# Attention with a maxout layer behind it on one core: q and k transposed by DMA from group 6 on, and the value product moved beside a score visit

## The chip, the core and the metric

The kernel runs on one of the eight cores of a Trainium2 chip. The time is the device time of one execution in microseconds (us), and lower is better. A core has five engines that run their own instruction streams and wait for one another through semaphores: TensorE (PE in the profile, its weight loads PEld), VectorE (DVE), ScalarE (ACT), GpSimd (POOL) and SyncE (SP). [...]

## The reference

Eight batches, twelve heads, 448 positions, head size 64. Softmax has one extra term in its denominator. What comes out is put side by side over the heads and goes through a layer that takes the largest of three products, and through an output product:

```
scores = (1/8) * q @ k.T            # (8, 12, 448, 448)
m      = max(scores)                # per row
e      = exp(scores - m)
attn   = e / (sum(e) + exp(-m) + 1e-9)
x      = attn @ v                   # put together as (3584, 768)
h      = max(x @ w1, x @ w2, x @ w3)
out    = h @ w_out                  # (3584, 768), float32
```

Times m, numerator and denominator become exp(scores) and sum(exp(scores)) + 1; the kernel computes those, without the maximum.

## The kernel before

**Groups.** The work is cut into 24 groups of four heads, three groups to a batch. The order of all instructions is the order in which the code calls them; nothing reorders it. One turn of the main loop (`for i in range(NI)`) does, on TensorE, the four score visits of group i, the value product of group i-1, the transposes of group i+1, and in between as many pieces of the maxout layer as a budget in columns allows (`moe`, line 281).

**One group.** `load_group` (line 76) has POOL load q, k and v as fp16, 112 positions to a chunk, into a pool of five buffers each. `pair_qk` (line 123) copies k and q of two heads side by side on VectorE, four copies to a group. `transpose_pair` (line 138) turns such a pair on TensorE: eight transposes of 112 by 128 into one PSUM bank, `trT`, and one VectorE copy to `qkT` in SBUF. `scores_visit` (line 152) does four products of 64 by 128 by 448 into `stp`, and ScalarE takes two exponentials of them into `eT`. `av_group` (line 179) does 48 products with 32 columns each: 16 with a matrix of ones for the denominator and 32 with v; ScalarE takes the logarithm and the exponential that make the reciprocal `rb`, and VectorE multiplies into `xT` (line 206, two per group).

**The maxout layer.** As soon as a batch's third group has its `xT`, `add_pieces` puts 18 pieces `up_piece` (six products of 128 by 128 by 448, then one VectorE copy or maximum into `hT`) and six or eight pieces `out_piece` (six products with 384 columns, one VectorE scaling into `o_sb`, and stores from SP) on a list. They fill the gaps of the next three groups.

**What is shared.** TensorE works in three arrangements of its array: whole (layer, transposes), two row halves (scores), four column strips (value product). PSUM has four single banks (`bank1`) for `trT`, `av`, `p_i` and `op_ps`, and two double ones for the scores. In the first turns POOL also loads the four weight matrices, between the groups.

Of the kernel before, what the change touches and what calls it, by code (L numbers as in the profile page):

```python
# [14 lines left out]
ts = bass.ts  # L15

MMDT = FP16
# [4 lines left out]
def kernel(  # L22
# [11 lines left out]
    nc = tc.nc  # L34

    B, H, S, D = q.shape
    NTOK, DM = out.shape
    DFF = moe_w1.shape[1]
    SC = 112
    NCH = S // SC  # L40
# [10 lines left out]
            name=nc.get_next_instruction_name(),  # L51
# [5 lines left out]

    cpool = ctx.enter_context(tc.tile_pool(name="const", bufs=1))
    ld_pool = ctx.enter_context(tc.tile_pool(name="ld", bufs=5))
    p16_pool = ctx.enter_context(tc.tile_pool(name="p16", bufs=2))  # L60
    att_pool = ctx.enter_context(tc.tile_pool(name="att", bufs=4))
    e_pool = ctx.enter_context(tc.tile_pool(name="e", bufs=2))
    small = ctx.enter_context(tc.tile_pool(name="small", bufs=2))
    xt_pool = ctx.enter_context(tc.tile_pool(name="xt", bufs=2))
# [11 lines left out]
    def load_group(i, which="qkv", step=GH):  # L76
        b, g = groups[i]
        tiles = raw.setdefault(i, {})
        for name in which:
            tiles[name] = ld_pool.tile(  # L80
                [SC, GH, NCH, D], MMDT, tag="ld_" + name, name="ld_" + name
            )
        for h0 in range(0, GH, step):
            for name in which:
                src = {"q": q, "k": k, "v": v}[name][b].rearrange(
                    "(g h) (p c) d -> g p h (c d)", g=NG, c=NCH
                )[g]
                nc.gpsimd.dma_start(  # L88
                    out=tiles[name][:, h0 : h0 + step].rearrange("p h c d -> p h (c d)"),
                    in_=src[:, h0 : h0 + step],  # L90
                )
# [19 lines left out]
    def load_weight(i):  # L111
        w = (moe_w1, moe_w2, moe_w3, moe_w_out)[i]
        for g in range(NG):
            if i < 3:
                src = w.rearrange("(g p hf) f -> g p hf f", g=NG, hf=2)[g]
            else:
                src = w.rearrange("(g hf p) f -> g p hf f", g=NG, hf=2)[g]
            nc.gpsimd.dma_start(out=w_sb[i][:, 2 * g : 2 * g + 2, :], in_=src)


    state = {}

    def pair_qk(i):
        qf, kf = raw[i].pop("q"), raw[i].pop("k")
        qk16 = []
        for pr in range(GH // 2):
            q16 = p16_pool.tile([SC, NCH, 2, D], MMDT, tag=f"q16_{pr}", name=f"q16_{pr}")
            k16 = p16_pool.tile([SC, NCH, 2, D], MMDT, tag=f"k16_{pr}", name=f"k16_{pr}")
            nc.vector.tensor_copy(
                out=k16, in_=kf[:, 2 * pr : 2 * pr + 2].rearrange("p h c d -> p c h d")  # L130
            )
            nc.vector.tensor_copy(
                out=q16, in_=qf[:, 2 * pr : 2 * pr + 2].rearrange("p h c d -> p c h d")
            )
            qk16.append((q16, k16))
        state[i] = {"qk16": qk16, "qkT": []}

    def transpose_pair(i, pr):
        st = state[i]
        q16, k16 = st["qk16"][pr]  # L140
        trT = ps1.tile([128, 2, S], MMDT, tag="bank1", name="trT")
        for n, t16 in enumerate((k16, q16)):
            for c in range(NCH):
                nc.tensor.transpose(  # L144
                    out=trT[:, n, ts(c, SC)], in_=t16[:, c, :, :],
                    identity=ident16[0:SC, 0:SC],
                )
        qkT = att_pool.tile([2 * D, 2 * S], MMDT, tag="qkT", name="qkT")
        nc.vector.tensor_copy(out=qkT, in_=trT.rearrange("p n s -> p (n s)"))  # L149
        st["qkT"].append(qkT)  # L150

    def scores_visit(i, pr, cs):
        st = state[i]
        if "eT" not in st:
            st["eT"] = e_pool.tile([SC, GH, NCH, S], MMDT, tag="eT", name="eT")
        qkT = st["qkT"][pr]
        stps = []
        for c in cs:
            stp = ps2.tile([128, 2, 512], FP32, tag="bank2", name="stp")
            for hh in range(2):  # L160
                nc.tensor.matmul(  # L161
                    out=stp[:, hh, 0:S],
                    lhsT=qkT[hh * D : hh * D + D, c * SC : c * SC + 128],
                    rhs=qkT[hh * D : hh * D + D, S : 2 * S],
                    start=True,
                    stop=True,
                )
            stps.append(stp)
        for c, stp in zip(cs, stps):
            nc.scalar.activation(  # L170
                out=st["eT"][:, 2 * pr : 2 * pr + 2, c, :],
                in_=stp[0:SC, :, 0:S],
                func=AF.Exp,
                scale=scale,
            )
# [3 lines left out]
    def av_group(i):  # L179
        b, g = groups[i]  # L180
        st = state.pop(i)
        eT, v16 = st["eT"], raw[i].pop("v")
        if g == 0:
            xT[b] = xt_pool.tile([128, NDC, S], MMDT, tag="xT", name="xT")

        def col_tiled(weights):
            bank = ps1.tile([128, 512], FP32, tag="bank1", name="av")
            for c in range(NCH):
                for hh in range(GH):
                    nc.tensor.matmul(  # L190
                        out=bank[32 * hh : 32 * hh + 32, 0:S],
                        lhsT=weights(hh, c),
                        rhs=eT[:, hh, c, :],
                        start=(c == 0),
                        stop=(c == NCH - 1),
                    )
            return bank

        den = col_tiled(lambda hh, c: ones16[:, :])
        lnd = small.tile([128, S], FP32, tag="lnd", name="lnd")  # L200
        nc.scalar.activation(out=lnd, in_=den[:, 0:S], func=AF.Ln, bias=one_b)  # L201
        rb = small.tile([128, S], FP32, tag="rb", name="rb")
        nc.scalar.activation(out=rb, in_=lnd, func=AF.Exp, bias=ln_lam, scale=-1.0)  # L203
        for hf in range(2):
            num = col_tiled(lambda hh, c: v16[:, hh, c, hf::2])
            nc.vector.tensor_tensor(  # L206
                out=xT[b][:, 2 * g + hf, :], in0=num[:, 0:S], in1=rb, op=ALU.mult
            )
# [60 lines left out]
    def add_pieces(b):  # L269
        order = [(fc, i) for fc in range(NFC) for i in range(3)]  # L270
        if b == 0:
            order = [(fc, i) for i in range(3) for fc in range(NFC)]
        for fc, i in order:
            pieces.append((up_piece, (b, fc, i), NDC * (S + 6)))
        for t in range(0, 3) if b % 2 == 0 else range(3, 7):
            for nh in range(NH):
                pieces.append((out_piece, (b // 2, t, nh), NFC * (NW + 6)))
# [3 lines left out]
    def moe(cols):  # L281
        credit[0] += cols
        while pieces and credit[0] > 0:
            f, a, w = pieces.pop(0)
            f(*a)
            credit[0] -= w
        if not pieces:
            credit[0] = min(credit[0], 0.0)
# [4 lines left out]
    per_group = (3 * NFC * UP + 3.5 * NH * OUT) / NG  # L293
    av_cols = 3 * NCH * (S + 6) + 480
    tr_cols = 2 * NCH * SC
    gap = (per_group + av_cols + 2 * tr_cols) / 4
    visits = [(pr, cs) for pr in range(2) for cs in ((0, 1), (2, 3))]
    NI = len(groups)

    pair_qk(0)  # L300
    transpose_pair(0, 0)
    transpose_pair(0, 1)

    for i in range(NI):
        b, g = groups[i]
        if i == 0:
            load_weight(0)
            load_group(3, "qk")
        elif i == 1:
            load_weight(1)  # L310
            load_group(3, "v")
        elif i == 2:
            load_weight(2)
            load_group(4)
            load_weight(3)
            load_group(5)
        elif i + 3 < NI:
            load_group(i + 3)
        for vi, (pr, cs) in enumerate(visits):
            scores_visit(i, pr, cs)  # L320
            if vi == 0:
                spare = gap - av_cols
                moe(spare / 2)
                if i > 0:
                    av_group(i - 1)
                moe(spare / 2)
                if i > 0 and g == 0:
                    add_pieces(b - 1)
                if i + 1 < NI:
                    pair_qk(i + 1)  # L330
            elif vi < 3:
                moe((gap - tr_cols) / 2)
                if i + 1 < NI:
                    transpose_pair(i + 1, vi - 1)
                moe((gap - tr_cols) / 2)
            else:
                moe(gap)
    av_group(NI - 1)
    add_pieces(B - 1)
# [31 lines left out]
```

## Time and profile before

| | |
|---|---|
| three runs | 378.81, 380.77 and 381.11 us, median 380.77 |
| profiled execution | 379.41 us, its span 377.6 us |
| TensorE busy | 358.3 us, 95% of the span |
| VectorE, ScalarE busy | 194.7 and 194.5 us, 52% each |
| GpSimd busy | 59.4 us, 16% |
| loads on POOL's queue | 21.24 MB, 40.8% of the sixteen DMA engines' span |
| stores on SP's queue | 11.01 MB, 9.8% |

Busy times overlap between engines. A matmul's span in the profile is longer than the step from one matmul to the next, since they are pipelined; the chain of waits, which follows the work that ended last back to the start, gives each piece of work by what it adds to the end.

### The profile page before, as it was taken

How to read it: one execution, taken by the hardware profiler on the slowest of the kernel's cores; microseconds unless marked ns; L12 is line 12 of the kernel's file. 1: busy time of each engine (PE TensorE's matmuls, PEld its weight loads, DVE VectorE, ACT ScalarE, POOL GpSimd, SP SyncE). 2: the span in 40 equal slices, each digit the busy share in tenths (PEclk: the TensorE clock that was granted, in tenths of full speed). 3: DMA queues.
4: the chain of work that ended last, by engine and by line, in shares of the span. 5: the costliest groups of instructions: out<-in, count | busy, mean ns of one | idle time of the engine just before them, and what ended most of it. 6: DMA issues, size and time to landing. Idle time of an engine off the chain costs nothing.

```text
span 377.6 us, 7320 instructions
## 1 busy us (share of the span) xinstructions
PE 358.3 (95%) x3120; PEld 172.0 (46%) x3120; DVE 194.7 (52%) x395; ACT 194.5 (52%) x241; POOL 59.4 (16%) x92
## 2 busy tenths in 40 slices
PE   2777999999999999999999999999999999999995
PEld 1233444544445444454445544454444554445552
DVE  2233545545546546546546555455465465445553
ACT  1879464663655655555555645546555554552000
POOL 8533450220210201202202202202000000000000
PEclk9999999999999999999999999999999999999999
DMA  7999998555508625455236555077010410013005
GB/s 92 185 208 206 204 196 121 73 136 68 73 2 151 111 54 75 60 139 75 32 43 89 126 101 73 6 128 141 2 26 0 128 43 0 2 32 95 2 0 168
DMA packets 40064, 32.71 MB, mean 87 GB/s; under 512 B 2272, under 2 KB 35296, under 8 KB 40032
## 3 DMA queue, kind: packets, MB, share of 16 engines
q0 software_dynamic: 35552, 21.24, 40.8%
q1 hardware_dynamic: 4480, 11.01, 9.8%
q8 instruction: 24, 0.39, 0.5%
q14 instruction: 8, 0.07, 0.0%
HBM read 42.47 MB, written 11.01 MB: 142 GB/s over the span
## 4 chain that ended last, share of the span: by engine, by line
PE 84%; DMA 9%; ACT 2%; POOL 2%; DVE 1%; issue 1%; DVEq 0%; POOLq 0%
PE p_i L220 43%; PE op_ps L241 15%; PE av L190 11%; PE stp L161 10%; PE trT L144 4%; DMA w_123<-in_moe_w_dram 3%; DMA ld_k<-in_k_dram 3%; DMA ld_q<-in_q_dram 2%; DVE xT L206 1%; ACT eT L170 1%; ACT rb L203 1%; ACT lnd L201 1%; POOL ld_q L88 1%; POOL ld_k L88 1%; POOL ld_v L88 0%
## 5 line engine op out<-in xcount | busy, mean ns | idle before, releaser
L170 ACT ACTIVATE eT<-stp 112x896 f16<-112x896 f32 x192 | 164.9, 916 | 145.1 <-PE stp L161 145.1
L230 DVE TENSOR_TENSOR hT<-hT,p_i 128x448 f16<-128x448 f16 x96 | 59.4, 619 | 45.5 <-PE p_i L220 45.1
L206 DVE TENSOR_TENSOR xT<-av,rb 128x448 f16<-128x448 f32 x48 | 27.8, 619 | 70.8 <-ACT rb L203 64.7
L220 PE MATMUL p_i<-xT,w_122 128*128 128x448 f16 x288 | 63.0, 353 | 0.4
L220 PE MATMUL p_i<-xT,w_123 128*128 128x448 f16 x288 | 62.4, 353 | 0.0
L220 PE MATMUL p_i<-xT,w_124 128*128 128x448 f16 x288 | 62.2, 353 | 0.0
L161 PE MATMUL stp<-qkT 64*128 64x448 f16 x384 | 56.3, 364 | 4.9 <-ACT eT L170 4.8
L241 PE MATMUL op_ps<-w_125,hT 128*128 128x384 f16 x336 | 59.5, 326 | 0.0
L88 POOL DMA_DIRECT2D ld_v<-in_v_dram x24 | 16.8, 702 | 192.3 <-PE av L190 126.3
L248 DVE TENSOR_SCALAR o_sb<-op_ps 128x384 f32<-128x384 f32 x56 | 31.2, 557 | 28.5 <-PE op_ps L241 28.4
L241 PEld LDWEIGHTS <-hT 128*128 128x128 f16 x336 | 30.9, 98 | 24.8 <-issue 6.3
L190 PE MATMUL av<-eT,ld_v 112*32 112x448 f16 x768 | 41.8, 361 | 0.0
L228 DVE CAST hT<-p_i 128x448 f16<-128x448 f32 x48 | 29.7, 620 | 19.9 <-PE p_i L220 19.9
L220 PEld LDWEIGHTS <-w_123 128*128 128x128 f16 x288 | 25.9, 98 | 29.6 <-issue 9.2
L220 PEld LDWEIGHTS <-w_124 128*128 128x128 f16 x288 | 26.0, 98 | 28.7 <-issue 7.8
L220 PEld LDWEIGHTS <-w_122 128*128 128x128 f16 x288 | 26.1, 98 | 27.8 <-issue 7.0
L149 DVE COPY qkT<-trT 128x896 f16<-128x896 f16 x48 | 29.5, 615 | 3.1 <-PE trT L144 3.0
L161 PEld LDWEIGHTS <-qkT 64*128 64x128 f16 x384 | 12.0, 94 | 40.9 <-issue 40.3
L190 PEld LDWEIGHTS <-ld_v 112*32 112x32 f16 x768 | 21.0, 99 | 16.8 <-issue 1.7
L190 PE MATMUL av<-eT,ones_116 112*32 112x448 f16 x384 | 23.3, 364 | 0.0
L88 POOL DMA_DIRECT2D ld_q<-in_q_dram x25 | 17.7, 709 | 6.9 <-DMA w_124<-in_moe_w_dram 1.5
L88 POOL DMA_DIRECT2D ld_k<-in_k_dram x25 | 17.6, 703 | 4.4 <-DMA w_123<-in_moe_w_dram 1.1
(305 smaller groups left out, 142.1 us busy)
## 6 DMA issues: line engine op xcount, KB each, us to landing
ld_v<-in_v_dram POOLq DMA_DIRECT2D x24, 224.0 KB, 4.0
ld_q<-in_q_dram POOLq DMA_DIRECT2D x23, 224.0 KB, 4.9
ld_k<-in_k_dram POOLq DMA_DIRECT2D x23, 224.0 KB, 5.9
out_dram<-o_sb SPq DMA_DIRECT2D x8, 336.0 KB, 2.8
out_dram<-o_sb SPq DMA_DIRECT2D x8, 288.0 KB, 2.7
out_dram<-o_sb SPq DMA_DIRECT2D x8, 240.0 KB, 2.8
out_dram<-o_sb SPq DMA_DIRECT2D x8, 192.0 KB, 2.7
w_122<-in_moe_w_dram POOLq DMA_DIRECT2D x3, 384.0 KB, 10.7
```

What stands on the lines that cost most here:

```text
L88: nc.gpsimd.dma_start(out=tiles[name][:, h0 : h0 + step].rearrange("p h c d -> p h (c d)"), in_=src[:, h0 : h0 + step],)
L144: nc.tensor.transpose(out=trT[:, n, ts(c, SC)], in_=t16[:, c, :, :], identity=ident16[0:SC, 0:SC],)
L149: nc.vector.tensor_copy(out=qkT, in_=trT.rearrange("p n s -> p (n s)"))
L161: nc.tensor.matmul(out=stp[:, hh, 0:S], lhsT=qkT[hh * D : hh * D + D, c * SC : c * SC + 128], rhs=qkT[hh * D : hh * D + D, S : 2 * S], sta ...
L170: nc.scalar.activation(out=st["eT"][:, 2 * pr : 2 * pr + 2, c, :], in_=stp[0:SC, :, 0:S], func=AF.Exp, scale=scale,)
L190: nc.tensor.matmul(out=bank[32 * hh : 32 * hh + 32, 0:S], lhsT=weights(hh, c), rhs=eT[:, hh, c, :], start=(c == 0), stop=(c == NCH - 1),)
L206: nc.vector.tensor_tensor(out=xT[b][:, 2 * g + hf, :], in0=num[:, 0:S], in1=rb, op=ALU.mult)
L220: nc.tensor.matmul(out=p_i[:, 0:S], lhsT=w_sb[i][:, dc, ts(fc, 128)], rhs=xT[b][:, dc, :], start=(dc == 0), stop=(dc == NDC - 1),)
L228: nc.vector.tensor_copy(out=dst, in_=p_i[:, 0:S])
L230: nc.vector.tensor_tensor(out=dst, in0=dst, in1=p_i[:, 0:S], op=ALU.max)
L241: nc.tensor.matmul(out=op_ps[:, 0:NW], lhsT=hT[bp][:, fc, ts(t, 128)], rhs=wout_sb[:, fc, ts(nh, NW)], start=(fc == 0), stop=(fc == NFC - 1),)
L248: nc.vector.tensor_scalar(out=o_sb[:, ts(nh, NW)], in0=op_ps[:, 0:NW], scalar1=1.0 / LAMBDA, scalar2=None, op0=ALU.mult,)
```

## The change

For groups 6 to 23 the eight TensorE transposes per pair, the PSUM bank and the VectorE copy out of it are gone. In their place SP issues one transposing DMA per pair, from the paired copy `qk16` in SBUF straight to `qkT`, 112 by 1024 elements; it is issued two groups ahead of the score visits that read it. k and q of a pair now lie in one tile. The pools are deepened: four pairs of `qk16` instead of two, six `qkT` instead of four. Groups 0 to 5 are transposed on TensorE as before. Inside a turn two things move: `pair_qk` now stands right behind the first score visit, ahead of the value product, and in turn 4 both group 5 and group 6 are paired there; and the value product stands right ahead of the second score visit, with the first gap's layer pieces before it. The budget `gap` is smaller by the transposes that are gone.

```
-    p16_pool = ctx.enter_context(tc.tile_pool(name="p16", bufs=2))
-    att_pool = ctx.enter_context(tc.tile_pool(name="att", bufs=4))
+    p16_pool = ctx.enter_context(tc.tile_pool(name="p16", bufs=4))
+    att_pool = ctx.enter_context(tc.tile_pool(name="att", bufs=6))
...
+            qk16 = p16_pool.tile([SC, 2, NCH, 2, D], MMDT, tag="qk16", name="qk16")
+            for n, t in enumerate((kf, qf)):
+                nc.vector.tensor_copy(
+                    out=qk16[:, n],
+                    in_=t[:, 2 * pr : 2 * pr + 2].rearrange("p h c d -> p c h d"),
+                )
...
+    def dma_transpose_pair(i, pr):
+        st = state[i]
+        qkT = att_pool.tile([2 * D, 2 * S], MMDT, tag="qkT", name="qkT")
+        nc.sync.dma_start_transpose(
+            out=qkT.rearrange("p (n s) -> p n s", s=SC),
+            in_=st["qk16"][pr].rearrange("p n c h d -> p (n c h d)"),
+        )
+        st["qkT"].append(qkT)
...
+        on_pe = i + 1 < PE_TR
+        tr = tr_cols if on_pe else 0
+        gap = (per_group + av_cols + 2 * tr) / 4
         for vi, (pr, cs) in enumerate(visits):
+            if vi == 1 and i > 0:
+                av_group(i - 1)
             scores_visit(i, pr, cs)
             if vi == 0:
-                spare = gap - av_cols
-                moe(spare / 2)
-                if i > 0:
-                    av_group(i - 1)
-                moe(spare / 2)
-                if i > 0 and g == 0:
+                if on_pe:
+                    pair_qk(i + 1)
+                if i + 2 >= PE_TR and i + 2 < NI:
+                    pair_qk(i + 2)
+                    for p2 in range(2):
+                        dma_transpose_pair(i + 2, p2)
+                moe(gap - av_cols)
+            elif vi < 3:
+                if vi == 1 and i > 0 and g == 0:
                     add_pieces(b - 1)
-                if i + 1 < NI:
-                    pair_qk(i + 1)
-            elif vi < 3:
-                moe((gap - tr_cols) / 2)
-                if i + 1 < NI:
-                    transpose_pair(i + 1, vi - 1)
-                moe((gap - tr_cols) / 2)
+                moe((gap - tr) / 2)
+                if on_pe:
+                    pe_transpose_pair(i + 1, vi - 1)
+                moe((gap - tr) / 2)
```

VectorE in turn 3, where the value product of group 2 completes the first batch and group 4 is paired. Before, the two multiplications into `xT`, then the four copies of group 4, then the first layer pieces:

```order
L206 TENSOR_TENSOR xT<-av,rb 128x448 x2
L129 COPY k_0_563<-ld_k 112x512
L132 COPY q_0_562<-ld_q 112x512
L129 COPY k_1_567<-ld_k 112x512
L132 COPY q_1_566<-ld_q 112x512
L228 CAST hT<-p_i 128x448 x2
```

The same place in the changed kernel (lines are those of its own file):

```order
L129 COPY qk_497<-ld_k 112x512
L129 COPY qk_497<-ld_q 112x512
L129 COPY qk_500<-ld_k 112x512
L129 COPY qk_500<-ld_q 112x512
L212 TENSOR_TENSOR xT<-av,rb 128x448 x2
L234 CAST hT<-p_i 128x448 x2
```

The four copies, which wait for the loads of group 4, now stand ahead of the two multiplications.

SP's queue of the changed kernel from its start (before, it held the stores alone): the transposes of groups 6 and 7, the first six stores, then the transposes of group 8.

```order
L152 DMA_TRANSPOSE qkT<-qk_692 128x8x112
L152 DMA_TRANSPOSE qkT<-qk_695 128x8x112
L152 DMA_TRANSPOSE qkT<-qk_885 128x8x112
L152 DMA_TRANSPOSE qkT<-qk_888 128x8x112
L270 DMA out_dram<-o_sb 112x768
L270 DMA out_dram<-o_sb 16x768
L270 DMA out_dram<-o_sb 96x768
L270 DMA out_dram<-o_sb 32x768
L270 DMA out_dram<-o_sb 80x768
L270 DMA out_dram<-o_sb 48x768
L152 DMA_TRANSPOSE qkT<-qk_1064 128x8x112
L152 DMA_TRANSPOSE qkT<-qk_1067 128x8x112
```

A transpose that waits now holds the stores behind it, and a store that waits holds the transposes.

More of the change, by code (lines that the diff above doesn't have):

```diff
@@ L124, in pair_qk, with pe_transpose_pair @@
         qf, kf = raw[i].pop("q"), raw[i].pop("k")
-        qk16 = []
+        state[i] = {"qk16": [], "qkT": []}
         for pr in range(GH // 2):
[L127 to L138, printed above, removed]
+            qk16 = p16_pool.tile([SC, 2, NCH, 2, D], MMDT, tag="qk16", name="qk16")
[4 more added lines that the diff above has]
+                )
+            state[i]["qk16"].append(qk16)
+    def pe_transpose_pair(i, pr):
         st = state[i]
-        q16, k16 = st["qk16"][pr]
+        qk16 = st["qk16"][pr]
         trT = ps1.tile([128, 2, S], MMDT, tag="bank1", name="trT")
-        for n, t16 in enumerate((k16, q16)):
+        for n in range(2):
             for c in range(NCH):
                 nc.tensor.transpose(
-                    out=trT[:, n, ts(c, SC)], in_=t16[:, c, :, :],
+                    out=trT[:, n, ts(c, SC)], in_=qk16[:, n, c, :, :],
                     identity=ident16[0:SC, 0:SC],
@@ L295 @@
     tr_cols = 2 * NCH * SC
-    gap = (per_group + av_cols + 2 * tr_cols) / 4
     visits = [(pr, cs) for pr in range(2) for cs in ((0, 1), (2, 3))]
     NI = len(groups)
+    PE_TR = 6
     pair_qk(0)
-    transpose_pair(0, 0)
-    transpose_pair(0, 1)
+    pe_transpose_pair(0, 0)
+    pe_transpose_pair(0, 1)
     for i in range(NI):
```

## The prediction

> **What bounds the kernel now.** I read the page first: busy time, the slices, the chain of waits.
>
> ```profile
> span 377.6 us, 7320 instructions
> PE   2777999999999999999999999999999999999995
> PE 84%; DMA 9%; ACT 2%; POOL 2%; DVE 1%; issue 1%; DVEq 0%; POOLq 0%
> PE p_i L220 43%; PE op_ps L241 15%; PE av L190 11%; PE stp L161 10%; PE trT L144 4%; DMA w_123<-in_moe_w_dram 3%; DMA ld_k<-in_k_dram 3%; DMA ld_q<-in_q_dram 2%; DVE xT L206 1%; ACT eT L170 1%; ACT rb L203 1%; ACT lnd L201 1%; POOL ld_q L88 1%; POOL ld_k L88 1%; POOL ld_v L88 0%
> ```
>
> TensorE is the bound from the fifth slice on, and the transposes stand on its chain with 4%. The DMA share is at the start. I then asked for the chain in order of time, once for the start (columns: start, length, what) and once for a turn in the middle.
>
> ```profile
> 29.02 12.52 DMA ld_k<-in_k_dram
> 41.63 0.30 DVE k_0_563 L129
> 41.98 0.57 PE trT L144 x8
> 42.55 1.14 PE p_i L220 x6
> 50.95 0.48 PE stp L161 x4
> ```
>
> ```profile
> 173.06 0.40 PE trT L144 x8
> 173.46 1.14 PE p_i L220 x6
> 174.59 0.48 PE stp L161 x4
> 175.08 1.24 PE p_i L220 x6
> 176.32 0.40 PE trT L144 x8
> 176.71 1.14 PE p_i L220 x6
> ```
>
> So there are two stages. Until 41.5 us the end is set by loads: the last to matter is k of group 4, issued at 29.02 and there at 41.54. Whatever TensorE gains before that is absorbed. From 42 us on TensorE goes from piece to piece without a hole, and what is taken out of its stream comes out of the time.
>
> **The change part by part.**
>
> *TensorE without transposes.* Groups 6 to 23 are 18, with two pairs each: 36 pairs. Their transposes and copies are all that lies between 68 and 350 us (columns: stretch, its length, busy time and count for line 144; then the same for the copy of line 149):
>
> ```profile
> 68.00:350.00 282.00, 20.11 (x288) 17.72 (x288) 1.00 0.40 70
> 68.00:350.00 282.00, 22.09 (x36) 1.00 0.40 70
> ```
>
> 288 is 36 x 8. Their 20.11 us of busy time overlaps itself, so the price is the chain's: 0.40 us per pair, and a layer piece costs the same 1.14 with a transpose behind it (173.46) as behind its own kind, since both use the whole array. Pieces alternate between 0.39 and 0.40; 36 x 0.395 = 14.2 us go. The 22.1 us of VectorE copies go too, but that engine was half idle and they are worth nothing by themselves.
>
> *The value product moved.* A change of arrangement costs about 0.10: a layer piece of 1.14 is 1.24 where a score visit follows. What counts is how many there are. By the order of the two programs there are 200 changes between whole array, row halves and column strips before, and 199 after: where the product stood behind the first visit it now stands ahead of the second. That the neighbour doesn't matter the end of the loop shows:
>
> ```profile
> 335.35 3.03 PE op_ps L241 x18
> 338.38 0.48 PE stp L161 x4
> 338.87 3.03 PE op_ps L241 x18
> 341.90 0.90 PE av L190 x16
> ```
>
> 18 output products take 3.03 ahead of scores and ahead of a value product. I take zero.
>
> *VectorE's copies ahead of the multiplications.* This is a new wait. In turn 3 the trace has:
>
> ```profile
> 38.88 1.16 DVE L206 TENSOR_TENSOR xT<-av,rb 128x448 f16<-128x448 f32 x2 [4.90 <-ACT rb L203]
> 39.22 2.44 PE L220 MATMUL p_i<-xT,w_122 128*128 128x448 f16 x12
> 41.63 0.29 DVE L129 COPY k_0_563<-ld_k 112x512 f16<-112x512 f16 x1 [1.60 <-DMA ld_k<-in_k_dram]
> 41.98 0.37 PE L144 MATMUL trT<-ident_97,k_0_563 112*128 112x112 f16 x4 [0.32 <-DVE k_0_563 L129]
> 42.45 1.14 DVE L228 CAST hT<-p_i 128x448 f16<-128x448 f32 x2
> ```
>
> The multiplications finish xT of the first batch at 40.04, and TensorE does two layer pieces while VectorE waits for k of group 4. In the changed kernel the four copies stand first and VectorE takes its queue in order, so the multiplications wait for the same load. The copies take until 42.45 (where the next operation started), the two multiplications 1.16, so xT is complete at 43.61, about 43.65 for TensorE. The first piece can do its first four products before that, its sixth at 43.65; that product takes 0.19 (a sixth of 1.14), the second piece 1.14, the transposes behind it 0.39: 45.37. Before, the same point is 42.55. So +2.8 us, and nothing later gives it back, since TensorE has no holes from there on. The load itself I take as unmoved, because POOL's order of loads is the same.
>
> In turn 4, from 50.95 (then 53.8), VectorE copies groups 5 and 6. Group 6's k is there at 54.3, by the time from its issue at 43.0 to landing:
>
> ```profile
> L88 POOL DMA_DIRECT2D ld_k<-in_k_dram x1: 701/701/701, 43.0 to 43.0; - x1
> DMA to landing us min/median/max: 11.3/11.3/11.3
> ```
>
> Group 5's copies cover those 0.5 us: zero. Without the delay in turn 3 it would have been a stall of its own. Later loads are there a turn or more ahead. In turns that begin a batch the copies also pass ahead of the multiplications, but these start 3.4 us after the first visit (166.98, then 170.37, below) and the copies are done by then.
>
> ```profile
> 166.98 0.55 PE L161 MATMUL stp<-qkT 64*128 64x448 f16 x4
> 170.37 1.15 DVE L206 TENSOR_TENSOR xT<-av,rb 128x448 f16<-128x448 f32 x2 [2.72 <-ACT rb L203]
> ```
>
> In that wait TensorE stands still for about 3 us (39.98 to 43.0). At the start of the trace its products ran at half pace:
>
> ```profile
> 17.67 1.69 PE L190 MATMUL av<-eT,ones_116 112*32 112x448 f16 x16
> 27.82 0.94 PE L190 MATMUL av<-eT,ones_116 112*32 112x448 f16 x16
> ```
>
> Sixteen of the 48 products took 0.75 longer there. If the pause brings that back for the length of one value product, it costs 3 x 0.75 = 2.2 us once; below, nothing. No row has a pause of this length after full pace. I take zero, because most of the trace's holes leave the pace alone (the product at 27.82 follows a stretch in which TensorE waited for ScalarE again and again), and keep 2.2 for the range. The Trainium skill (TensorE: Matmul & The Clock Gate, Part 1) has the clock fall to half after about 3.4 us without work; by that rule this pause is just too short.
>
> *The transposing DMAs.* No row shows one. Each moves 112 x 1024 fp16, the 224 KB of one load. A turn is 14.58 us long before: turn 4 begins at 50.95 and turn 23 at 327.90 (row further down), 276.95 / 19. Two pairs fewer make it 13.79. Group 6's transposes are issued at about 55.9 (53.8, the visit, eight copies) and read about 82, two turns after turn 4. After that SP needs two in every turn, so sustained a transpose may take 6.9 us. Bounds from rows: a load of that size lands in 4.0 us, and in the 11.3 above where the engines are full.
>
> ```profile
> ld_v<-in_v_dram POOLq DMA_DIRECT2D x24, 224.0 KB, 4.0
> w_123<-in_moe_w_dram POOLq DMA_DIRECT2D x3, 384.0 KB, 13.6
> 51.00:66.00 15.00, 15.00 (x136) 6.82 (x134) 8.37 (x17) 8.19 (x11) 3.50 (x5) 1.00 1.11 150
> 124.00:167.00 43.00, 43.00 (x388) 20.75 (x379) 23.75 (x48) 23.81 (x30) 6.29 (x9) 1.00 0.48 78
> ```
>
> The last two rows are stretches; the second number from the end is the DMA share, 1.11 until 66 us and 0.48 later. The steady stage has room, so I take about 4 us, under 6.9, and a cost of zero. VectorE's copies two groups on and SP's stores queue behind these DMAs; at 4 us they are free eight us after the first visit, before the stores need SP.
>
> Sum: 379.41 - 14.2 + 2.8 = 368.0 against the profiled execution. The median of the runs is 1.36 above that execution: **369.4**.
>
> **The rivals.**
>
> *The transposes are too slow (slower).* They run one after another in SP's queue, and with a time T each the 35th ends at 55.9 + 35 T; the first visit of turn 23, at 327.90 before (the visit behind the row at 325.82), would be at 316.5 after.
>
> ```profile
> 325.82 2.08 PE p_i L220 x11
> 327.90 0.48 PE stp L161 x4
> ```
>
> Up to T = 7.45 this costs nothing, at 7.8 the gain of 11.4 is gone, and at the 11.3 of a load under full engines the end is 135 us later: 369.4 + 135 = 504. It makes no difference whether SP or the DMA engines take the time. For it: T is unseen, and full engines do reach it. Against: the share of 0.48. The Trainium skill (VectorE: DVE Perf Modes, The three transpose paths) gives 1309 ns for 128 by 128 by DMA against 390 by TensorE; eight blocks in series would be 10.5 us, an estimate from that page, and the time about 476. It speaks against the change. The skill's DMA: Bandwidth & Descriptors (Latency and other measured facts) has 261 GB/s, which would be 0.9 us. No run here shows either.
>
> *Only the first ones are slow.* The engines are full until about 66 us. If the four transposes of groups 6 and 7 take the 13.6 of a weight load each, the fourth ends at 110.3; it is read about 102.2: the visit ends at 101.88 before, by the piece behind it, so it begins at 101.40, 2.8 later by turn 3 and 2.0 earlier by five pairs.
>
> ```profile
> 101.88 1.24 PE p_i L220 x6
> ```
>
> That is 8.1 later: 377.5. For it: the row of 1.11. Against: it needs the worst landing four times, three of them after the engines have emptied.
>
> *The load doesn't hold VectorE.* If group 4's k lands 2.8 us earlier, the full 14.2 stays: 366.6. Against: nothing ahead of it on POOL moves.
>
> **How the numbers follow.** Forecast (366.6 to 372, its upper end with the slow clock) 0.55; load not in the way 0.13; first ones slow 0.10; too slow 0.22, of which 0.03 ends inside 1%. About 1% is what a measurement here tells from no change: 377.0 to 384.6 around the median before. The case at 377.5 lies near that edge and I halve it. Faster: 0.55 + 0.13 + 0.05 = 0.73. Same: 0.05 + 0.03 = 0.08. Slower: 0.19. The range 365.5 to 382 holds the first three cases and a little of the fourth, about 0.8.
>
> **What would show it.** Right: 96 transposes left on line 141 and none behind turn 4; the chain goes score visit, layer piece, score visit with no transpose; VectorE waits for DMA in turn 3 and xT is done near 43.6; weight loads of line 167 never wait for a DMA; a turn near 13.8. Wrong: TensorE idle until a `qkT` DMA; a transpose over 7 us in the list of DMA issues; SP or VectorE waiting for transposes; the layer slower per piece than 1.14.

## The result and the profile after

The changed kernel takes 367.82 us (median of three executions, 367.40 to 369.71), against 380.13 for the kernel before in the runs beside it: a ratio of 0.969 (of the means), with a 95% interval of 0.963 to 0.975. A fourth execution, the profiled one, had a granted TensorE clock of 0.85 and took 408.79 us; with it the median is 368.76, whose nearness to the forecast of 369.4 is therefore chance, and the profile shown here is that of a repeat. The repeat, with five executions, gave 367.64 against 380.60, 0.968 (0.965 to 0.970).

The page of the changed kernel, its slices, its DMA queues and its chain of waits:

```profile
span 365.6 us, 6789 instructions
PE 345.7 (95%) x2832; PEld 158.6 (43%) x2832; DVE 176.2 (48%) x359; ACT 195.7 (54%) x241; POOL 59.4 (16%) x92
PE   2777899999999999999999999999999999999994
q1 hardware_dynamic: 37888, 19.28, 23.9%
PE 83%; DMA 9%; ACT 2%; DVE 2%; POOL 2%; issue 1%; DVEq 0%; POOLq 0%
PE p_i L226 45%; PE op_ps L247 16%; PE av L196 11%; PE stp L167 10%; DMA ld_k<-in_k_dram 3%; DMA w<-in_moe_w_dram 3%; DMA ld_q<-in_q_dram 2%; DVE xT L212 2%; ACT eT L176 1%; ACT rb L209 1%; ACT lnd L207 1%; POOL ld_q L88 1%; POOL ld_k L88 1%; PE trT L141 0%; POOL ld_v L88 0%
```

TensorE has 288 matmuls fewer (2832 against 3120), VectorE 36 copies fewer, and the transposes have gone from 4% of the chain to under one half. SP's queue moved 19.28 MB instead of 11.01; TensorE is still the bound.

Turn 3 of the changed kernel in order of time:

```profile
39.26 0.55 PE L167 MATMUL stp<-qkT 64*128 64x448 f16 x4
39.74 0.93 PE L226 MATMUL p_i<-xT,w 128*128 128x448 f16 x4
40.41 0.29 DVE L129 COPY qk<-ld_k 112x512 f16<-112x512 f16 x1 [5.53 <-DMA ld_k<-in_k_dram]
41.22 1.15 DVE L212 TENSOR_TENSOR xT<-av,rb 128x448 f16<-128x448 f32 x2
41.89 0.35 PE L226 MATMUL p_i<-xT,w 128*128 128x448 f16 x1 [1.22 <-DVE xT L212]
42.42 1.48 PE L226 MATMUL p_i<-xT,w 128*128 128x448 f16 x7 [0.18 <-DVE xT L212]
```

This is the new wait, step by step as it was forecast: VectorE stands 5.5 us in front of the copies, which wait for group 4's load; then come the two multiplications, and TensorE, after four products, waits for each of them. Around the end of the main loop the chain of waits has:

```profile
312.70 0.48 PE stp L167 x4
313.19 2.38 PE p_i L226 x12
315.56 0.48 PE stp L167 x4
316.05 1.24 PE p_i L226 x6
317.29 2.38 PE av L196 x48
319.67 0.48 PE stp L167 x4
```

A layer piece is followed by score visits and value products alone, with no transpose, and at the prices of before: 1.14 and 0.10 for the change of arrangement, 2.38, 0.48. The transposing DMAs, from the list of DMA issues (us from issue to landing) and from the rows of line 152 (time that SP itself was held, in ns: smallest, median, largest):

```profile
qkT<-qk SPq DMA_TRANSPOSE x36, 3.2
L152 SPq DMA_TRANSPOSE qkT<-qk x36: 1222/1239/2414, 54.7 to 290.6; - x36
DMA to landing us min/median/max: 2.6/3.2/9.4
```

A median of 3.2 us, 1.24 of it SP's own. No engine is listed as having waited for a `qkT` DMA. The first pair, issued while the DMA engines were full, took 7.7 and 9.4 us, and VectorE waited twice for a store to free `o_sb` (2.0 us in all), which it did not before; neither stands on the chain.

### The profile page after: what moved, and what is told of

It reads as the page before. It is cut to its first block, busy times and chain, and to the rows that moved or that the text cites. A ratio compares the mean times of both kernels' runs of the same rounds, so it can differ in the third digit from the quotient of the medians.

```text
span 407.0 us, 6789 instructions
## 1 busy us (share of the span) xinstructions
PE 389.1 (96%) x2832; PEld 167.4 (41%) x2832; DVE 176.1 (43%) x359; ACT 196.4 (48%) x241; POOL 59.4 (15%) x92
## 3 DMA queue, kind: packets, MB, share of 16 engines
q1 hardware_dynamic: 37888, 19.28, 20.7%
HBM read 42.47 MB, written 11.01 MB: 131 GB/s over the span
## 4 chain that ended last, share of the span: by engine, by line
PE 92%; ACT 3%; DMA 2%; POOL 1%; issue 0%; DVE 0%; POOLq 0%
PE p_i L226 48%; PE av L196 17%; PE op_ps L247 16%; PE stp L167 11%; ACT eT L176 3%; DMA ld_k<-in_k_dram 2%; PE trT L141 1%; POOL ld_q L88 1%; POOL ld_k L88 0%; DVE o_sb L254 0%; DVE qk_170 L129 0%; POOL ident_97 masks.py:199 0%; POOL ident_97 masks.py:197 0%; POOLq L366 0%
## 5 line engine op out<-in xcount | busy, mean ns | idle before, releaser
L226 PE MATMUL p_i<-xT,w_122 128*128 128x448 f16 x288 | 70.8, 387 | 0.0
L226 PE MATMUL p_i<-xT,w_123 128*128 128x448 f16 x288 | 70.7, 388 | 0.0
L226 PE MATMUL p_i<-xT,w_124 128*128 128x448 f16 x288 | 70.2, 387 | 0.0
L247 PE MATMUL op_ps<-w_125,hT 128*128 128x384 f16 x336 | 66.5, 358 | 0.0
L167 PE MATMUL stp<-qkT 64*128 64x448 f16 x384 | 59.9, 385 | 5.5 <-ACT eT L176 5.4
L196 PE MATMUL av<-eT,ld_v 112*32 112x448 f16 x768 | 49.5, 408 | 0.0
L247 PEld LDWEIGHTS <-hT 128*128 128x128 f16 x336 | 33.7, 104 | 32.4 <-issue 7.1
L226 PEld LDWEIGHTS <-w_123 128*128 128x128 f16 x288 | 28.6, 104 | 35.3 <-issue 7.3
L226 PEld LDWEIGHTS <-w_124 128*128 128x128 f16 x288 | 27.7, 103 | 36.4 <-issue 9.3
L226 PEld LDWEIGHTS <-w_122 128*128 128x128 f16 x288 | 27.9, 103 | 35.5 <-issue 7.9
L196 PEld LDWEIGHTS <-ld_v 112*32 112x32 f16 x768 | 22.5, 108 | 22.7 <-issue 4.3
L196 PE MATMUL av<-eT,ones_116 112*32 112x448 f16 x384 | 25.6, 393 | 0.0
L207 ACT ACTIVATE lnd<-av,one_b 128x448 f32<-128x448 f32 x24 | 15.3, 638 | 14.9 <-PE av L196 14.8
```

The lines of the kernel that those rows point to most:

```text
L167: nc.tensor.matmul(out=stp[:, hh, 0:S], lhsT=qkT[hh * D : hh * D + D, c * SC : c * SC + 128], rhs=qkT[hh * D : hh * D + D, S : 2 * S], sta ...
L196: nc.tensor.matmul(out=bank[32 * hh : 32 * hh + 32, 0:S], lhsT=weights(hh, c), rhs=eT[:, hh, c, :], start=(c == 0), stop=(c == NCH - 1),)
L226: nc.tensor.matmul(out=p_i[:, 0:S], lhsT=w_sb[i][:, dc, ts(fc, 128)], rhs=xT[b][:, dc, :], start=(dc == 0), stop=(dc == NDC - 1),)
L247: nc.tensor.matmul(out=op_ps[:, 0:NW], lhsT=hT[bp][:, fc, ts(t, 128)], rhs=wout_sb[:, fc, ts(nh, NW)], start=(fc == 0), stop=(fc == NFC - 1),)
```

## The experiments

**The change again.**

> The changed kernel as it is. By the prediction's sum 368.0 profiled, some 3% under the kernel before: 14.2 us less TensorE work and 2.8 us of a new wait in turn 3, where TensorE should stand still from about 40 to 43 us until the two multiplications into xT have followed the four copies of group 4. If the wait is not there (the rival in which the load doesn't hold VectorE), TensorE shows no hole between 39 and 44 us and the whole 14.2 us shows in the time, about 366.6.

Measured: 367.64 us (367.32 to 367.76). The hole is there, as the rows above show, so the rival in which the load doesn't hold VectorE falls.

**The copies behind the value product again.** The pairing and the DMA issue stand behind `av_group`, all else as in the changed kernel.

```
...
             if vi == 1 and i > 0:
                 av_group(i - 1)
+                if on_pe:
+                    pair_qk(i + 1)
+                if i + 2 >= PE_TR and i + 2 < NI:
+                    pair_qk(i + 2)
+                    for p2 in range(2):
+                        dma_transpose_pair(i + 2, p2)
             scores_visit(i, pr, cs)
             if vi == 0:
-                if on_pe:
-                    pair_qk(i + 1)
...
```

> The changed kernel with one thing undone: pair_qk and the issue of the transposing DMAs stand behind the value product again, so that VectorE's multiplications pass ahead of the copies that wait for a load. If the new wait costs 2.8 us, this is 2.8 us faster than the changed kernel (a ratio to before of about 0.962 against 0.969) and layer pieces run in turn 3 before group 4's k is there. If the order of VectorE's queue costs nothing, the two are equal.

Measured: 366.44 us (365.79 to 367.78), ratio 0.965 (0.962 to 0.968). That is 1.2 us under the changed kernel, in the direction forecast and less than half its size. Its turn 3:

```profile
39.40 1.16 DVE L212 TENSOR_TENSOR xT<-av,rb 128x448 f16<-128x448 f32 x2 [4.52 <-ACT rb L209]
39.75 2.44 PE L226 MATMUL p_i<-xT,w 128*128 128x448 f16 x12
40.75 0.29 DVE L129 COPY qk<-ld_k 112x512 f16<-112x512 f16 x1 [0.19 <-DMA ld_k<-in_k_dram]
42.03 0.56 PE L141 MATMUL trT<-ident,qk 112*128 112x112 f16 x8
```

The hole is gone: TensorE runs its two pieces while the load arrives.

**The transposing DMAs alone**, with the kernel before's order of a turn.

```
-            if vi == 1 and i > 0:
-                av_group(i - 1)
             scores_visit(i, pr, cs)
             if vi == 0:
+                spare = gap - av_cols
+                moe(spare / 2)
+                if i > 0:
+                    av_group(i - 1)
+                moe(spare / 2)
+                if i > 0 and g == 0:
+                    add_pieces(b - 1)
                 if on_pe:
                     pair_qk(i + 1)
...
```

> The kernel before with the transposing DMAs from group 6 alone: the value product and the copies stay where they were in the turn. By the sum 14.2 us under before (ratio 0.963), and equal to the run with the copies behind the product, since moving the value product is taken at zero. If the moved value product is itself worth something, the run with the copies behind is faster than this one.

Measured: 366.75 us (365.19 to 369.06), ratio 0.967 (0.963 to 0.970): 13.85 under the 380.60 of the runs beside it, with an interval of 11.4 to 14.1. Forecast was 14.2. It is within 0.3 us of the run with the copies behind the product: the place of the value product is worth nothing that can be measured.

**The order alone**, every transpose on TensorE.

```
-    PE_TR = 6
+    PE_TR = 24
```

> The order of the changed kernel's turn with every transpose left on TensorE. By the sum 2.8 us above before (ratio 1.007): nothing is taken away, and the wait in turn 3 is added. If the order costs nothing, the ratio is 1.000; if it is worth something by itself, it is under 1.

Measured: 381.76 us, ratio 1.0044 (1.0023 to 1.0064): 0.9 to 2.4 us slower. So the new order costs something whether the DMAs are there or not, and less than 2.8.

**No transposes from group 6 on.**

```
...
-        qkT = att_pool.tile([2 * D, 2 * S], MMDT, tag="qkT", name="qkT")
-        nc.sync.dma_start_transpose(
-            out=qkT.rearrange("p (n s) -> p n s", s=SC),
-            in_=st["qk16"][pr].rearrange("p n c h d -> p (n c h d)"),
-        )
-        st["qkT"].append(qkT)
+        st["qkT"].append(fixed[pr])
...
```

`fixed` holds the two transposed pairs of group 5.

> No transposes at all from group 6 on: the transposing DMAs are left out and the scores of groups 6 to 23 read the transposed pairs of group 5 (the copies on VectorE stay). It shows what the DMAs themselves cost. By the prediction nothing: the same time as the changed kernel. If they slow the loads, hold SP or make TensorE wait, this is faster than the changed kernel by as much.

Measured: 367.45 us (366.95 to 367.74) against 367.64 with the DMAs. The two runs stand beside 380.40 and 380.60 of the kernel before. The DMAs cost nothing that can be measured.

**Every transpose twice.** The same call again, into a tile that nothing reads.

> Every transposing DMA is issued twice, the second time into a tile that nothing reads: four per turn on SP. The profile of the changed kernel has about 1.24 us of SP per transpose and 2.6 to 6.5 us from issue to landing, so four take about 5 us of SP and at most 16 us in series of a slack of two turns (27 us): the same time as the changed kernel. If the queue runs one transpose after the other at 4 us or more, four would take over 16 us a turn against 13.8, and the time would rise by 18 x 2.2 = 40 us.

Measured: 368.27 us, ratio 0.968 (0.966 to 0.970). The 0.6 us above the changed kernel are within what these medians can differ by. Doubling the load on the queue leaves the time where it was, though the median landing rose from 3.2 to 4.6 us.

**One group ahead instead of two**, the copies with the transposes.

> The transposes one group ahead instead of two. With landings of 2.6 to 6.5 us, an issue about 2 us after a turn begins is there well before the next turn 13.8 us later: the same time as the changed kernel. It would be slower if the second turn of slack is needed, by TensorE waiting for a qkT DMA.

Measured: 368.04 us, ratio 0.968 (0.965 to 0.970). Its waits name a `qkT` DMA three times (us in total, times, longest), but with no weight:

```profile
PEld L167 <- DMA qkT<-qk: 1.1, 3, 0.4
```

So the second turn of slack isn't needed in the steady stage.

**From group 3 instead of group 6** (`PE_TR = 3`).

> The DMA transposes begin with group 3 instead of group 6, while the DMA engines are full with loads. Three more groups would save 6 x 0.395 = 2.4 us of TensorE if nothing waits. But group 3's loads and group 4's land at about 28 and 41.5 us, VectorE takes its copies in order, and pairing two groups ahead makes the first multiplications wait for the load of a group one turn further on: group 5's k, at 50.7 us, ahead of the first batch's xT. Then layer pieces start about 9 us later than in the kernel before: expected 5 to 8 us slower than the changed kernel. If the order on VectorE doesn't matter, it is about 2.4 us faster.

Measured: 385.50 us, ratio 1.014 (1.012 to 1.017): 18 us slower than the changed kernel, more than twice the 5 to 8 expected. VectorE does wait for the loads one turn further on, as expected (the last row: 8.6 us for group 5's, and 18.2 us for group 4's one turn earlier), but there is a second wait, of TensorE for the DMA transpose itself:

```profile
43.41 0.93 PE L167 MATMUL stp<-qkT 64*128 64x448 f16 x4 [5.07 <-DMA qkT<-qk]
47.29 0.29 DVE L129 COPY qk<-ld_k 112x512 f16<-112x512 f16 x1 [18.21 <-DMA ld_k<-in_k_dram]
57.86 0.29 DVE L129 COPY qk<-ld_k 112x512 f16<-112x512 f16 x1 [8.62 <-DMA ld_k<-in_k_dram]
```

The first two transposes took 16.9 and 19.3 us from issue to landing, and the load of group 4 was there at 47.2 instead of 40.3. Behind these waits the granted clock was 0.50 for several us at a time (from 59.35 us thirteen products of the layer took 5.17 us, 0.40 each instead of 0.19), which is part of the 18.

**From group 3, one turn ahead for groups 3 to 5**, to part the two waits.

```
-    PE_TR = 6
+    PE_TR = 3
...
+                if 3 <= i + 1 < 6:
+                    pair_qk(i + 1)
+                    for p2 in range(2):
+                        dma_transpose_pair(i + 1, p2)
-                if i + 2 >= PE_TR and i + 2 < NI:
+                if i + 2 >= 6 and i + 2 < NI:
```

> DMA transposes from group 3, but groups 3 to 5 are paired and transposed one turn ahead, so that VectorE waits for the same loads as in the changed kernel. It parts two causes of the 18 us that the start from group 3 cost. If that was VectorE waiting for a load one turn further on, this is about as fast as the changed kernel, or 2.4 us faster. If it was the transposes themselves, which took 17 to 19 us to land there while the loads filled the DMA engines, TensorE still waits for them: one turn of slack (about 10 to 14 us) is too short, and each of groups 3 and 4 costs several us: 375 to 385.

Measured: 374.17 us (373.89 to 374.58): a little under the range expected, 6.5 above the changed kernel and 11.3 under the start from group 3 with two turns. Both waits are real. With VectorE's order out of the way, TensorE still stands 9.3 us for the first pair, and the next load is as late as in the run before:

```profile
26.42 35.99 SPq L152 DMA_TRANSPOSE qkT<-qk  x5
43.65 0.93 PE L167 MATMUL stp<-qkT 64*128 64x448 f16 x4 [9.31 <-DMA qkT<-qk]
44.51 1.69 PE L196 MATMUL av<-eT,ones 112*32 112x448 f16 x16
47.38 0.29 DVE L129 COPY qk<-ld_k 112x512 f16<-112x512 f16 x1 [15.91 <-DMA ld_k<-in_k_dram]
```

The third row is the value product behind that wait. Its first sixteen products took 1.69 us instead of 0.94, at a granted clock of 0.50.

**Every transpose seven times.**

> Every transposing DMA seven times, six of them into a tile that nothing reads: it looks for the limit of the slack. SP takes 1.24 us for each, so a pair takes 8.7 us of SP, and by the prediction's formula the 35th pair ends at 55.9 + 35 x 8.7 = 360 against 316.5: 43 us slower than the changed kernel, about 411, with SP busy from end to end and TensorE waiting for DMA. If the DMA engines are the tighter limit, it is slower than that; if the transposes' price is neither, it is nearer to the changed kernel.

Measured: 553.6 us, ratio 1.456 (1.446 to 1.466): far beyond 411. The limit exists, and it is tighter than SP's 1.24 us by itself. The first transposes of the 36 pairs went out between 54.4 and 488.8 us, 12.4 us from pair to pair, or 1.77 us for each transpose with the stores between them. With 12.4 per pair the formula of the prediction gives 55.9 + 35 x 12.4 = 490 against 316.5, 173 us more, or 541. TensorE's granted clock averaged 0.85 in this run, with 0.7 in the stretches in which it stood most; how much that adds is not shown. The waits name what went with it: VectorE waits for a store to free `o_sb`, TensorE for VectorE, and VectorE's copies for the transposes that still read their source.

```profile
DVE qk L129 <- DMA spare<-qk: 112.5, 15, 16.3
DVE o_sb L260 <- DMA out_dram<-o_sb: 92.7, 3, 33.5
PE op_ps L253 <- DVE o_sb L260: 83.3, 3, 30.4
```

Stores that stand behind transposes in SP's queue stopped TensorE three times, for up to 30 us.

**Group 4's q and k loaded ahead of the third weight matrix**, in the changed kernel, and once more with the copies behind the value product.

```
-            load_weight(2)
-            load_group(4)
+            load_group(4, "qk")
+            load_weight(2)
+            load_group(4, "v")
             load_weight(3)
```

> The changed kernel with q and k of group 4 loaded ahead of the third weight matrix, so that the copies have nothing to wait for in turn 3. If the cost of the new order is that wait, it goes: 1.2 us faster than the changed kernel and equal to the run with the copies behind, with no hole of TensorE at 40 to 42 us. If it is something else of the order, the time stays.

> The copies behind the value product, as in the run that was 1.2 us faster than the changed kernel, and q and k of group 4 loaded ahead of the third weight matrix. If the start is still set by that load, this is faster than the run with the copies behind, by up to 1 us; if it is set by ScalarE and TensorE from the start on, the two are equal.

Measured: 365.11 us (364.94 to 367.08) for the changed kernel with the load moved, ratio 0.962 (0.959 to 0.964), and 367.14 (366.19 to 367.83) with the copies behind as well. The first is 2.5 us under the changed kernel, which was measured in another round (beside 380.60 of the kernel before, this one beside 380.48), and the fastest kernel of this study. Its copies pass at 35 us, and TensorE waits for nothing in turn 3:

```profile
35.03 0.29 DVE L129 COPY qk<-ld_k 112x512 f16<-112x512 f16 x1 [0.38 <-DMA ld_k<-in_k_dram]
36.72 4.07 PE av L196 x48
40.79 0.48 PE stp L167 x4
41.27 2.38 PE p_i L226 x12
```

So the wait goes with the load, which was its cause. The gain is twice the 1.2 that was expected, and the time is under that of the run with the copies behind (366.44), not equal to it; where the rest comes from is not shown. That the second is 2.0 us slower than the first was not expected either. The profiled execution of the first was its slowest (367.08) and has the same span as the other's, 365.3 us; in it the granted clock was 0.50 twice in the start stage, for 3.4 us each, and in the other's once. So their traces can't settle it. The second is no faster than the run with the copies behind (366.44) either, which fits that run's chain: up to turn 3 it goes through ScalarE and TensorE, not through that load. With the copies behind, the chain of that kernel goes through them in turn 2 (multiplications, copies, transposes, scores), which the other order avoids; whether that is the whole 2 us stays open.

## Why the prediction was right

**What bounds it: right.** Two stages, loads until about 41 us and TensorE after that.

**TensorE without transposes, -14.2: right.** In the medians it is -13.85 with the DMAs alone, where 14.2 lies at the edge of the interval. In the trace of the repeat the time from turn 4 to turn 23, which holds all 36 pairs, is 262.87 us against 276.95, 14.1 less. And the run without any transpose is no faster than the one with DMAs, so no part of it is given back.

**The value product moved, 0: right.** 366.44 with it moved and 366.75 without, the copies standing behind it in both.

**The copies ahead of the multiplications, +2.8: the mechanism right, the size too large.** It measured 1.2 us by two pairs of runs, with 0.9 to 2.4 as the interval of one. So the whole change is worth 14.2 - 1.2 = 13.0 us, as in the repeat, and not the 11.4 of the forecast. The steps of the working hold: xT complete 2.07 us after the load (43.61 from 41.54 forecast; 42.38 from 40.31 measured), the hole, the two pieces after it. What failed is the value under it. The load's landing at 41.54 was taken from one execution as if it were fixed; in the repeat it was there at 40.31:

```profile
27.81 12.50 DMA ld_k<-in_k_dram
42.42 1.48 PE p_i L226 x7
43.91 0.39 PE trT L141 x8
```

In the trace of before the load was so late that it held TensorE there as well. In the profile with the copies behind the load was 0.9 us sooner, and still the transposes were done at 42.59 and not before 42.55. There TensorE itself is the bound: the value product of turn 2 had taken it 4.07 us at a granted clock of 0.50, and it came to turn 3 half a us later than in the trace of before, where the clock was 1.00. The new order, which hangs on the load, has the transposes done at 44.30 instead of 45.37. The difference shrinks from 2.8 to 1.7 in the profiles and 1.2 in the medians. So the trace of before was one draw in two ways, the load's landing and the clock. A price that is the distance of two waits moves with the one that is not tied to the engine.

**The pause and the clock, 0: right, for a shorter pause than was weighed.** After the hole seven products took 1.48 us, their full pace (six take 1.30 right behind them), and the granted clock stayed at 1.00. The hole was 1.2 us and not 3, so this kernel did not put the longer pause to the test. The starts from group 3 did. In the one with one turn ahead TensorE stood for 9.3 us, the clock fell to 0.50 1.1 us after its last product, and the value product behind the wait took 4.60 us instead of 2.38: the 2.2 that the prediction kept for its range. In the one with two turns ahead the clock fell 1.5 and 3.3 us after the last product. So the 3.4 us of the Trainium skill (TensorE: Matmul & The Clock Gate, Part 1) were no safe bound in these traces, and that a pause of 3 us would have cost nothing is not shown.

**The DMAs, about 4 us and no cost: right.** 3.2 us in the median. The first pair, issued at 54.7 while the engines were full, took 7.7 and 9.4, inside the bounds of 4.0 and 11.3. A transpose over 7 us was among the prediction's signs of being wrong; these two and one of 7.3 at 84 us cost nothing, since what they write is read two turns later.

**A turn, 13.8: right.** Turn 4 begins at 52.69 and turn 23 at 315.56, so a turn is 262.87 / 19 = 13.84.

**The rivals.** That the transposes are too slow would have needed 7.45 us for a pair. In the steady stage a pair takes SP 1.24 us, and seven at once 1.77 each; the point is four times away. The Trainium skill's 1309 ns for a block of 128 by 128 (VectorE: DVE Perf Modes, The three transpose paths) doesn't add up over the blocks of one DMA: eight blocks landed in 2.6 to 3.4 us where the engines had room. The Trainium skill's 261 GB/s (DMA: Bandwidth & Descriptors, Latency and other measured facts) would be 0.9 us, an estimate from that page. The DMA rows of the two profiles give 1.4 us of all sixteen engines for each transpose (below), so no run here shows that rate. That only the first transposes are slow did not happen at group 6; at group 3, where it was provoked, it did, with 17 to 19 us.

## What to carry to other kernels

Work that is moved from a full engine to an idle queue pays its whole price if the queue's own time per turn (here two times 1.24 us of 13.8) leaves room and if the first uses come after the start, when the DMA engines are full. When a step is moved ahead in an in-order queue, look at what it waits for and who stands behind it: four small copies that wait for a load cost 1.2 us by standing in front of two multiplications, and issuing that load earlier gave it back and more. A load's landing in one trace is one draw, and so is TensorE's clock in the start stage; a difference that rests on them should carry their spread.

## What the runs showed that was not expected

Under full DMA engines a transposing DMA is as slow as the loads of the same size beside it, and makes them slower. In the two starts from group 3 the first transposes landed after 16.9 to 19.4 us, and the loads of group 4's q and k, issued next to them, after 19.0 to 19.4; in the changed kernel, with no transpose there, the same two loads took 13.2 and 12.5. The second transpose also held SP for 10.0 and 10.5 us. Group 4's k landed 7 us later than without them. In bytes and packets it is not remarkable: by the DMA rows of the profiles SP's queue had (37888 - 4480) / 36 = 928 packets more for each transpose, 247 bytes long, and (0.239 x 365.6 - 0.098 x 377.6) / 36 = 1.4 us of all sixteen engines.

In the start stage TensorE's pace changes from one execution to the next. The first sixteen products of turn 2's value product took 0.94 us in the trace of before and 1.38 in that of the repeat, where those of turn 3 took 0.94 again:

```profile
27.10 1.38 PE L196 MATMUL av<-eT,ones 112*32 112x448 f16 x16
36.88 0.94 PE L196 MATMUL av<-eT,ones 112*32 112x448 f16 x16
```

The granted clock goes with it: in the repeat it was 0.50 from 27.4 to 30.8 us and 1.00 on either side. TensorE had no hole longer than 0.5 us in the two us ahead of that, so a pause was not what set it off; what did is not shown. In the kernel with the load moved turn 2's and turn 3's products were slow (4.07 us for the 48 of turn 3 against 2.38). While a load sets the end of that stage this is hidden; with the load out of the way it is worth up to 1.7 us for each such stretch, about as much as the differences between the last few kernels here.
